# Warm-up matmuls: fifty of 256 columns for twenty-four of 512, in other banks and at one more place

## The chip, the cores and the metric

The kernel runs on one core of one Trainium2 chip. Its engines are TensorE (PE, with its weight loads listed as PEld), VectorE (DVE), ScalarE (ACT), GpSimd (POOL) and SyncE (SP), which here issues the DMAs. The metric is the device time of one execution in microseconds (us); lower is better.

## The reference

Two stages. First a gated linear attention over 768 steps for 4 batches of 8 heads with 48 channels: each head keeps a 48x48 state that is decayed by a sigmoid gate and takes in one outer product per step. Then a two-layer network on the 3072 tokens of 384 channels.

```python
def _attn_ref(q, k, v, f_logit):
    f = 1.0 / (1.0 + np.exp(-f_logit))
    state = np.zeros((B, H, D, D))
    for t in range(S):
        state = f[:, :, t, :, None] * state + np.einsum('bhd,bhe->bhde', k[:, :, t], v[:, :, t])
        y[:, :, t] = np.einsum('bhd,bhde->bhe', q[:, :, t], state)

def _moe_ref(x, w_in, w_out):
    h = x @ w_in                      # 3072 x 384 by 384 x 2048
    g = np.maximum(0.01 * h, h)
    return (g @ w_out)                # by 2048 x 384
```

## The kernel before, in words

The steps are cut into chunks of 128. There are twelve units of work: units 0 to 3 are the first two chunks of one batch each ("paired"), units 4 to 11 one later chunk of two batches. Each unit goes through the same steps:

- loads of f, k, q and v (`Lf`, `Lk`, `Lq`, `Lv`), all issued by SyncE in a fixed order;
- log gates on ScalarE (`ge` line 229, `gl` line 241);
- their prefix sums as matmuls with a triangular matrix (`cs`, lines 250 to 261), in paired units with a small addition on VectorE (`ca`, line 266);
- decay factors on ScalarE (`dec`, lines 274 to 280);
- k and q scaled by them (`k`, `q`, line 286) on VectorE or GpSimd, v cast on GpSimd (`v`, line 291);
- k and q turned, by transposes on TensorE (`tk`, `tq`, line 319) with copies on VectorE or ScalarE (`ck`, `cq`, lines 332 and 334), in later units by DMA (line 339);
- scores (`sc`, lines 355 and 362), masks on VectorE (`mk`, lines 372 and 376);
- the mix of scores and state (`mx`, `ms`, line 393) and the copy into xT (`xt`, lines 445 and 447);
- the state itself (`pt` line 458, `sf` lines 473 and 475, `sb` line 483);
- the network: up matmuls (`up` line 510 with 256 columns, `uw` line 521 with 512), the leaky ReLU on ScalarE (`pr`, `pw`, lines 516 and 525), down matmuls (`dn`, line 532), copies out and stores.

The two weight matrices are loaded in pieces (`We`, `WI`, `WO`) and cast to bf16 by three engines (`Ce`, `CI`, `CO`, lines 187 to 202).

Nothing schedules this at build time: one long list of words, `order`, is walked from left to right, and each word issues its step. So the list sets the order on every engine. A word such as `sc_1_0@6.7` says: the scores of unit 1, half 0, into PSUM banks 6 and 7. There are eight banks of 128 x 512 float32, given by hand. A step that writes a bank waits until the earlier contents have been read.

The word `F_7@1` means seven fills into bank 1. A fill (line 134) is a matmul of a constant tile with itself; nobody reads its result. Its bank counts like any other: the fill waits for the last reader of that bank.

Of the kernel before, what the change touches and what calls it, by code (L numbers as in the profile page):

```python
# [15 lines left out]
def kernel(  # L16
# [10 lines left out]
    nc = tc.nc  # L27
# [53 lines left out]
    banks = [psum.tile([128, 512], FP32, name=f"ps{i}", tag=f"ps{i}") for i in range(8)]  # L81
# [8 lines left out]
    filler = const.tile([128, 128], BF16, tag="filler")  # L90
# [40 lines left out]

    def fill(n, bank):
        for _ in range(n):
            nc.tensor.matmul(banks[bank].rearrange("t (a n) -> t a n", a=4), filler,  # L134
                             filler[:, None, :].to_broadcast([128, 4, 128]), start=True, stop=True)
# [349 lines left out]
    def wide(j):  # L485
        return j // 2 * 2 in WIDE
# [78 lines left out]
    def store(j, a):  # L565
# [46 lines left out]
    xt_5_1_1 mx_5_0@1 xt_5_0_1 dn_3_0_3 xt_4_0_0 uw_4_7@7 uw_4_9@4 pt_5_1@1 Lk_6_1 sf_4_1 ob_2_1_1 uw_4_4@2 pw_4_7
    Lf_8_0 Lk_6_0 uw_4_15@6 uw_4_0@7 pw_4_4 sf_4_0 uw_4_10@3 ob_3_1_0 uw_4_3@2 pw_4_9 pw_4_0 q_6_2_1 pw_4_10 ge_7_2
    uw_4_8@4 pt_5_0@7 sf_5_0 uw_4_12@5 uw_4_11@3 pw_4_3 uw_4_1@2 uw_4_2@7 pw_4_15 sb_4_1 gl_7_2 pw_4_8 pw_4_11 xq_6
    Lv_6_1 Lq_7_1 cs_7_1@6 cs_7_0@4 pw_4_1 pw_4_2 dec_7_1 uw_4_6@3 sb_5_0 sb_4_0 Lk_7_0 uw_4_13@2 sf_5_1 Lf_8_1
    Lq_7_0 dec_7_0 pw_4_6 st_1_0 k_6_2_0 pw_4_13 dn_4_1_0@1 uw_4_5@7 xk_6 q_7_2_0 pw_4_5 st_2_1 k_7_2_1 xk_7 Lv_6_0
# [64 lines left out]
```

## Time and profile before

| what | us |
|---|---|
| median of three runs | 179.84 |
| the three runs | 179.12, 179.84, 180.2 |
| the profiled execution, whole | 178.5 |
| its span, first to last instruction | 176.7 |
| TensorE busy in the span | 168.0 |
| ScalarE busy | 107.5 |
| VectorE busy | 79.1 |
| GpSimd busy | 72.7 |
| the 24 fills, busy | 9.2 |

The span is what the profile's rows are measured in; the whole execution is 1.8 us longer. An instruction is named by engine, line, operation and "out<-in" with tile names. PSUM banks all read `ps` there. Overlapping matmuls are pipelined, so a matmul's own duration is longer than the distance to the next one's start; costs of matmuls in a row are best read from the chain of waits, where each piece is only the time that it adds.

### The profile page before, as it was taken

How to read it: one execution, taken by the hardware profiler on the slowest of the kernel's cores; microseconds unless marked ns; L12 is line 12 of the kernel's file. 1: busy time of each engine (PE TensorE's matmuls, PEld its weight loads, DVE VectorE, ACT ScalarE, POOL GpSimd, SP SyncE). 2: the span in 40 equal slices, each digit the busy share in tenths (PEclk: the TensorE clock that was granted, in tenths of full speed). 3: DMA queues.
4: the chain of work that ended last, by engine and by line, in shares of the span. 5: the costliest groups of instructions: out<-in, count | busy, mean ns of one | idle time of the engine just before them, and what ended most of it. 6: DMA issues, size and time to landing. Idle time of an engine off the chain costs nothing.

```text
span 176.7 us, 5136 instructions
## 1 busy us (share of the span) xinstructions
PE 168.0 (95%) x2096; PEld 105.6 (60%) x2096; DVE 79.1 (45%) x166; ACT 107.5 (61%) x234; POOL 72.7 (41%) x151
## 2 busy tenths in 40 slices
PE   7698889999999999999999998999999999999993
PEld 2475668787566786754556744455754555644662
DVE  5259957802217333835128844506735355300030
ACT  4886964999155599269960687641799610378401
POOL 4687585532551745208525344802206980000000
PEclk9999999999999999999999999999999999999999
DMA  5999999499999499979999889999999990103004
GB/s 148 317 323 342 355 312 353 125 326 209 312 206 210 91 194 177 215 188 200 211 229 233 192 188 216 227 134 212 264 206 225 156 250 0 48 0 137 0 22 156
DMA packets 110407, 34.93 MB, mean 198 GB/s; under 512 B 102832, under 2 KB 109616, under 8 KB 110384
## 3 DMA queue, kind: packets, MB, share of 16 engines
q1 hardware_dynamic: 110384, 34.61, 84.1%
q8 instruction: 16, 0.26, 0.6%
q14 instruction: 7, 0.06, 0.1%
HBM read 25.17 MB, written 4.72 MB: 169 GB/s over the span
## 4 chain that ended last, share of the span: by engine, by line
PE 90%; DVE 3%; ACT 2%; DMA 2%; issue 1%; SPq 0%; DVEq 0%
PE ps L532 35%; PE ps L521 22%; PE ps L510 11%; PE ps L393 6%; PE ps L134 3%; PE ps L362 3%; DMA raw_fk<-in_f_logit_dram 2%; PE ps L319 2%; PE ps L548 2%; PE ps L258 1%; DVE wm L372 1%; PE ps L463 1%; PE ps L355 1%; PE ps L458 1%; PE ps L250 1%
## 5 line engine op out<-in xcount | busy, mean ns | idle before, releaser
L532 PE MATMUL ps<-w_out,gT 128*128 128x384 bf16 x368 | 66.1, 326 | 0.9 <-DVE sf L475 0.9
L532 PEld LDWEIGHTS <-gT 128*128 128x128 bf16 x368 | 34.4, 98 | 24.3 <-issue 1.2
L521 PE MATMUL ps<-xT,w_in 128*128 128x512 bf16 x192 | 45.2, 379 | 0.0
L525 ACT ACTIVATE gT<-ps 128x512 bf16<-128x512 f32 x64 | 34.5, 623 | 10.1 <-PE ps L521 9.6
L521 PEld LDWEIGHTS <-w_in 128*128 128x128 bf16 x192 | 18.1, 98 | 18.9
L376 DVE TENSOR_TENSOR wm<-ps,ut 128x512 bf16<-128x512 f32 x32 | 19.9, 684 | 17.0 <-PE ps L362 12.2
L286 POOL TENSOR_TENSOR qh<-raw_qv,at 128x768 bf16<-128x768 f32 (+1 forms) x10 | 14.0, 1404 | 24.3 <-ACT gT L525 9.4
L510 PE MATMUL ps<-xT,w_in 128*128 128x256 bf16 x192 | 22.9, 273 | 0.4 <-ACT xT L445 0.2
L516 ACT ACTIVATE gT<-ps 128x512 bf16<-128x512 f32 x32 | 17.9, 616 | 6.2 <-PE ps L510 6.2
L291 POOL CAST vb<-raw_qv 128x384 bf16<-128x384 f32 (+1 forms) x16 | 11.6, 723 | 23.6 <-DMA raw_qv<-in_v_dram 23.4
L510 PEld LDWEIGHTS <-w_in 128*128 128x128 bf16 x192 | 18.4, 98 | 3.6 <-DVE w_in L189 0.5
L483 POOL CAST sb<-sf 64x192 bf16<-64x192 f32 x40 | 14.9, 374 | 10.8 <-DVE sf L473 8.5
L445 ACT CAST xT<-ps 128x384 bf16<-128x384 f32 x15 | 7.8, 529 | 16.9 <-PE ps L393 13.5
L274 ACT ACTIVATE em<-ps 128x384 bf16<-128x384 f32 x24 | 12.2, 508 | 9.0 <-DVE wm L376 5.5
L229 ACT ACTIVATE e<-raw_fk 128x384 f32<-128x384 f32 (+1 forms) x16 | 11.0, 685 | 8.1 <-DMA raw_fk<-in_f_logit_dram 8.0
L286 DVE TENSOR_TENSOR kh<-raw_fk,em 128x768 bf16<-128x768 f32 (+1 forms) x10 | 9.0, 901 | 14.6 <-ACT em L274 9.7
L475 DVE TENSOR_TENSOR sf<-sf,ps 64x192 f32<-64x192 f32 x32 | 11.2, 351 | 6.4 <-ACT at L275 2.8
L543 DVE COPY osb<-ps 128x384 f32<-128x384 f32 x13 | 7.1, 554 | 13.0 <-PE ps L532 9.0
L275 ACT ACTIVATE at<-ps 128x384 bf16<-128x384 f32 x24 | 12.3, 512 | 0.0
L480 POOL TENSOR_TENSOR sf<-sf,end 128x192 f32<-128x192 f32 x16 | 8.9, 556 | 5.9 <-DVE sf L475 5.6
L372 DVE TENSOR_TENSOR wm<-ps,pair_mask 128x512 bf16<-128x512 f32 x16 | 10.4, 685 | 1.8 <-ACT lf L241 0.9
L134 PE MATMUL ps<-filler 128*128 128x512 bf16 x24 | 9.2, 511 | 2.0 <-DVE filler L93 1.1
(90 smaller groups left out, 180.2 us busy)
## 6 DMA issues: line engine op xcount, KB each, us to landing
out_dram<-osb SPq DMA_DIRECT2D x23, 192.0 KB, 3.1
raw_fk<-in_f_logit_dram SPq DMA_DIRECT2D x18, 192.0 KB, 3.8
raw_qv<-in_v_dram SPq DMA_DIRECT2D x18, 192.0 KB, 3.6
raw_fk<-in_k_dram SPq DMA_DIRECT2D x18, 192.0 KB, 3.7
raw_qv<-in_q_dram SPq DMA_DIRECT2D x18, 192.0 KB, 3.8
raw_fk<-in_moe_w_out_dram SPq DMA_DIRECT2D x2, 768.0 KB, 7.2
raw_qv<-in_moe_w_out_dram SPq DMA_DIRECT2D x2, 768.0 KB, 5.0
raw_fk<-in_f_logit_dram SPq DMA_DIRECT2D x3, 384.0 KB, 4.7
```

Source lines behind the costliest of these rows:

```text
L134: nc.tensor.matmul(banks[bank].rearrange("t (a n) -> t a n", a=4), filler, filler[:, None, :].to_broadcast([128, 4, 128]), start=True, sto ...
L274: nc.scalar.activation(ems[j % 2][:, a], t[:, 0:H * D], AF.Exp, scale=1.0)
L275: nc.scalar.activation(ats[j % 2][:, a], t[:, 0:H * D], AF.Exp, scale=-1.0)
L286: eng.tensor_mul(heads(j, to[j % NR], a)[:, :, :, 0:D], raw_heads(j, x, a), decays(j, by, a))
L372: nc.vector.tensor_mul(w.rearrange("t (s p) n -> t s p n", s=2), src.rearrange("t (s p n) -> t s p n", s=2, p=2), pair_mask[:, :, None, :] ...
L376: nc.vector.tensor_mul(w, src.rearrange("t (p n) -> t p n", p=P2), ut[:, None, :].to_broadcast([128, P2, 128]))
L483: nc.gpsimd.tensor_copy(out=sb[rows, :, y * D:y * D + D], in_=sf[rows])
L510: nc.tensor.matmul(pm[:, i, :], w_in_of(ff, kk), xTs[j // 2 % 2][:, kk, j % 2].rearrange("t a s -> t (a s)"), start=(kk == 0), stop=(kk == ...
L516: nc.scalar.activation(dst, pm, AF.Prelu, alpha=0.01)
L521: nc.tensor.matmul(banks[bank], w_in_of(ff, kk), xTs[j // 2 % 2][:, kk].rearrange("t u a s -> t (u a s)"), start=(kk == 0), stop=(kk == NK ...
L525: nc.scalar.activation(g_blocks(j)[ff], banks[st[j].pop(("pm", ff))], AF.Prelu, alpha=0.01)
L532: nc.tensor.matmul(po, g_of(j, ff, a), w_out_b[quarter][:, ff % 4, :], start=(ff == 0), stop=(ff == NF - 1))
```

## The change

A fill has 256 columns instead of 512. There are 50 fills instead of 24:

| place in the list, ahead of | before | after |
|---|---|---|
| first prefix sum of unit 0, `cs_0_1` | 7 in bank 1 | 21 in bank 1 |
| its second, `cs_0_0` | 3 in bank 2 | 3 in bank 2 |
| first of unit 1, `cs_1_0` | 3 in bank 3 | 5 in bank 3 |
| transposes `tk_1_1` | 4 in bank 5 | 7 in bank 4 |
| prefix sum `cs_2_1` | 2 in bank 1 | 3 in bank 3 |
| transposes `tq_1_0` | 1 in bank 4 | 2 in bank 4 |
| scores `sc_1_0` | 2 in bank 5 | 2 in bank 6 |
| mix `mx_1_2` | 2 in bank 2 | 3 in bank 5 |
| up matmuls `up_0_5` | none | 4 in bank 3 |

All other words stand in the same order. From `up_3_3` on, five of the eight banks are exchanged for each other (0 to 3, 1 to 2, 2 to 0, 3 to 5, 5 to 1), the same way to the end of the list; ahead of it only the fills' banks differ.

```diff
     def fill(n, bank):
         for _ in range(n):
-            nc.tensor.matmul(banks[bank].rearrange("t (a n) -> t a n", a=4), filler,
-                             filler[:, None, :].to_broadcast([128, 4, 128]), start=True, stop=True)
+            nc.tensor.matmul(banks[bank][:, 0:256].rearrange("t (a n) -> t a n", a=2), filler,
+                             filler[:, None, :].to_broadcast([128, 2, 128]), start=True, stop=True)
...
-    c0 Lf_0_1 ge_0_1 Lf_1_2 ge_1_1 gl_0_1 ge_1_0 zk_0 zv_0_0 zs_0_0 Lv_0_1 Lf_0_0 F_7@1 cs_0_1@0 ge_0_0 gl_0_0 Lk_0_1
+    c0 Lf_0_1 ge_0_1 Lf_1_2 ge_1_1 gl_0_1 ge_1_0 zk_0 zv_0_0 zs_0_0 Lv_0_1 Lf_0_0 F_21@1 cs_0_1@0 ge_0_0 gl_0_0
...
-    up_1_1@4 mk_2_0_1 sf_2_0 up_1_0@1 mk_2_1_1 Ce_1_0_1_1 pr_1_1 pr_1_0 mk_2_0_0 up_0_5@3 up_1_5@0 We_1_1 Lf_3_2
+    up_1_1@4 mk_2_0_1 sf_2_0 up_1_0@1 mk_2_1_1 Ce_1_0_1_1 pr_1_1 pr_1_0 mk_2_0_0 F_4@3 up_0_5@3 up_1_5@0 We_1_1
...
```

Three places as they stand in the program. In the rows `ps1_156` is bank 1 with a running number, `lf` the log gates, `bu` and `bs` the triangular matrices, `wm` the masked scores, `vb` the cast v, `kh` the scaled k, `w_in` the weights; `128x512` is the size of what is written.

TensorE, the last of the fills ahead of the first prefix sum and the first of those behind it, before:

```order
L134 LDWEIGHTS filler_170
L134 MATMUL ps1_156<-filler_170 128x512
L250 LDWEIGHTS bu_163
L250 MATMUL ps0_155<-lf0_78,bu_163 128x192
...
L255 MATMUL ps0_155<-half_ones_169,lf0_78 128x2
L134 LDWEIGHTS filler_170
L134 MATMUL ps2_157<-filler_170 128x512
```

The same place after the change:

```order
L134 LDWEIGHTS filler_170
L134 MATMUL ps1_156<-filler_170 128x256
L250 LDWEIGHTS bu_163
L250 MATMUL ps0_155<-lf0_78,bu_163 128x192
...
L255 MATMUL ps0_155<-half_ones_169,lf0_78 128x2
L134 LDWEIGHTS filler_170
L134 MATMUL ps2_157<-filler_170 128x256
```

The order is the same; the fills are half as wide, and the pair of weight load and fill is there 21 times instead of 7 ahead of `bu`.

TensorE, the fills between the state matmuls of unit 1 (L458) and its mix (L393), before:

```order
L458 MATMUL ps6_161<-vb1_96,kh1_82 128x96
L134 LDWEIGHTS filler_170
L134 MATMUL ps2_157<-filler_170 128x512
...
L393 LDWEIGHTS vb1_96
L393 MATMUL ps5_160<-wm4_109,vb1_96 32x128
```

After:

```order
L458 MATMUL ps6_161<-vb1_96,kh1_82 128x96
L134 LDWEIGHTS filler_170
L134 MATMUL ps5_160<-filler_170 128x256
...
L393 LDWEIGHTS vb1_96
L393 MATMUL ps5_160<-wm4_109,vb1_96 32x128
```

The fills went from bank 2, which held scores that a mask on VectorE reads, to bank 5, which held an earlier mix that ScalarE copied into xT and which the next mix writes.

TensorE, the up matmuls of unit 0 that read the third block of w_in, before:

```order
L510 LDWEIGHTS w_in0_171
L510 MATMUL ps1_156<-xT0_125,w_in0_171 128x256
L510 LDWEIGHTS w_in2_173
L510 MATMUL ps3_158<-xT0_125,w_in2_173 128x256
```

After:

```order
L510 LDWEIGHTS w_in0_171
L510 MATMUL ps1_156<-xT0_125,w_in0_171 128x256
L134 LDWEIGHTS filler_170
L134 MATMUL ps3_158<-filler_170 128x256
...
L510 LDWEIGHTS w_in2_173
L510 MATMUL ps3_158<-xT0_125,w_in2_173 128x256
```

Four fills now stand between the up matmuls on the first weight block and those on the third, in the bank that the latter write next.

More of the change, by code (lines that the diff above doesn't have):

```diff
@@ L612 @@
[L612 to L616, printed above, removed]
@@ new lines @@
+    pr_3_4 st_0_1 Lq_6_1 dn_2_1_3 v_4_2 ob_2_0_1 dn_3_1_1 cs_6_0@0 pr_3_7 v_5_2 dec_6_0 Lf_7_1 sc_5_0@2.5 sc_5_1@7.4
+    dn_3_1_2 mk_5_0_1 cs_6_1@5 mk_5_0_0 dn_3_0_0@3 dn_3_0_1 st_1_1 mk_5_1_0 sc_4_1@2.0 mk_5_1_1 sc_4_0@7.4 dec_6_1
+    mk_4_1_1 dn_3_0_2 pt_4_0@5 mk_4_1_0 mk_4_0_0 pt_4_1@0 dn_3_1_3 mk_4_0_1 mx_4_1@2 mx_4_0@7 mx_5_1@4 xt_4_1_1
+    xt_5_1_1 mx_5_0@2 xt_5_0_1 dn_3_0_3 xt_4_0_0 uw_4_7@7 uw_4_9@4 pt_5_1@2 Lk_6_1 sf_4_1 ob_2_1_1 uw_4_4@0 pw_4_7
+    Lf_8_0 Lk_6_0 uw_4_15@6 uw_4_0@7 pw_4_4 sf_4_0 uw_4_10@5 ob_3_1_0 uw_4_3@0 pw_4_9 pw_4_0 q_6_2_1 pw_4_10 ge_7_2
@@ new lines @@
+    dn_4_0_1 dn_4_1_1 dn_5_1_1 dn_4_0_2 sc_6_1@7.3 sc_6_0@1.0 Lf_11_1 dn_4_1_2 Lk_9_0 dn_4_1_3 mk_6_1_0 mk_6_1_1
+    mk_6_0_1 dn_5_0_1 dn_4_0_3 mk_6_0_0 ob_4_1_0 sc_7_1@7.3 sc_7_0@0.1 cs_8_0@2 dn_5_1_2 dn_5_0_2 Lv_8_1 mk_7_0_1
+    mk_7_0_0 mk_7_1_0 mk_7_1_1 cs_8_1@1 mx_6_1@0 dec_8_1 mx_6_0@7 mx_7_1@3 xt_6_0_0 mx_7_0@1 xt_7_1_0 pt_6_1@7
+    xt_6_1_1 xt_7_0_1 sf_6_1 dec_8_0 ge_9_2 sb_6_1 dn_5_0_3 pt_7_0@0 uw_6_14@3 uw_6_0@1 pw_6_0 pw_6_14 gl_9_2
+    uw_6_4@7 dn_5_1_3 uw_6_1@2 ob_5_1_0 pw_6_1 uw_6_8@1 cs_9_0@3 uw_6_3@5 pt_6_0@2 pw_6_4 sf_7_0 uw_6_2@0 ob_4_0_0
@@ new lines @@
+    pw_8_7 pw_8_0 pw_8_12 Lq_10_0 q_10_2_1 sb_9_0 v_10_2 pw_8_9 uw_8_10@3 Lv_11_1 Lq_11_0 Lk_11_1 st_7_0 uw_8_6@7
+    Lk_11_0 uw_8_11@1 uw_8_8@2 sf_9_1 k_10_2_0 uw_8_13@4 pw_8_8 pw_8_11 pw_8_10 pw_8_13 dn_8_0_0@6 xq_10 xk_10 sf_8_1
+    k_11_2_0 dn_9_1_0@5 dn_8_1_0@0 uw_8_15@2 q_11_2_1 pw_8_6 dn_9_1_1 dn_8_0_1 sc_10_0@1.3 sc_10_1@4.7 pw_8_15
+    dn_8_1_1 dn_8_0_2 xq_11 st_6_1 xk_11 dn_9_1_2 dn_9_0_0@2 dn_9_0_1 v_11_2 sb_8_0 sb_8_1 sb_9_1 st_7_1 mk_10_0_0
+    mk_10_1_0 mk_10_1_1 mk_10_0_1 sc_11_0@1.4 sc_11_1@7.3 dn_8_1_2 dn_8_0_3 dn_9_1_3 dn_9_0_2 mk_11_1_0 mk_11_0_1
@@ new lines @@
+    mk_11_0_0 mk_11_1_1 mx_11_1@7 mx_10_0@4 mx_10_1@1 mx_11_0@3 xt_11_1_1 dn_9_0_3 xt_10_1_0 xt_10_0_1 xt_11_0_1
+    ob_9_1_0 uw_10_8@7 uw_10_0@4 uw_10_2@1 dn_8_1_3 uw_10_5@3 pw_10_5 pw_10_0 ob_9_0_0 uw_10_6@5 pw_10_6 uw_10_4@2
+    uw_10_12@3 pw_10_4 uw_10_9@4 uw_10_1@5 st_6_0 uw_10_7@2 st_9_0 ob_8_0_1 uw_10_3@6 ob_8_1_1 pw_10_2 pw_10_8
+    pw_10_1 pw_10_7 uw_10_13@0 uw_10_10@1 pw_10_3 uw_10_11@7 uw_10_14@5 dn_11_0_0@2 st_8_1 st_8_0 pw_10_10 pw_10_11
+    pw_10_14 pw_10_13 pw_10_9 dn_10_0_0@6 uw_10_15@1 pw_10_12 dn_11_0_1 dn_10_1_0@7 dn_10_1_1 st_9_1 dn_10_0_1
```

67 lines of the change are left out of this document (26 added, 41 removed).

## The prediction

> **What bounds the kernel now.** I read the page first, then TensorE's timeline of the first 50 us, then the chain of waits up to 45 us, and last the timelines of ScalarE, VectorE and the DMA issues in the stretch where that chain leaves TensorE. From the page:
>
> ```profile
> span 176.7 us, 5136 instructions
> PEclk9999999999999999999999999999999999999999
> PE 90%; DVE 3%; ACT 2%; DMA 2%; issue 1%; SPq 0%; DVEq 0%
> L532 PE MATMUL ps<-w_out,gT 128*128 128x384 bf16 x368 | 66.1, 326 | 0.9 <-DVE sf L475 0.9
> L521 PE MATMUL ps<-xT,w_in 128*128 128x512 bf16 x192 | 45.2, 379 | 0.0
> L134 PE MATMUL ps<-filler 128*128 128x512 bf16 x24 | 9.2, 511 | 2.0 <-DVE filler L93 1.1
> ```
>
> TensorE carries 90% of the chain that ended last. The two big groups of real work, L532 and L521, lose 0.9 us in all to waits; so what moves the start of that work moves the end. The 24 fills (L134) compute nothing that is used. All the waits that matter are early:
>
> ```profile
> 1.05 3.17 PE L134 MATMUL ps<-filler 128*128 128x512 bf16 x7 [1.05 <-DVE filler L93]
> 5.80 0.32 PE L250 MATMUL ps<-lf,bu 128*128 128x192 bf16 x1 [1.57 <-ACT lf L241]
> ...
> 20.67 0.59 PE L134 MATMUL ps<-filler 128*128 128x512 bf16 x2 [0.50 <-DVE wm L372]
> ```
>
> Seven fills keep TensorE busy from 1.05 to 4.22; then it idles 1.57 us until the first log gates are there. The chain of waits (start, length, what) shows what follows:
>
> ```profile
> 5.33 0.42 ACT lf L241
> ...
> 6.68 1.30 PE ps L134 x3
> 7.98 0.16 PE ps L250
> 8.14 0.16 PE ps L251
> ...
> 8.71 1.29 PE ps L134 x3
> 10.00 0.08 PE ps L250
> 10.08 0.08 PE ps L251
> ...
> 20.67 0.59 PE ps L134 x2
> ...
> 22.03 0.60 ACT xT L445
> ...
> 23.43 0.45 issue
> ...
> 26.39 4.04 PE ps L510 x36
> ...
> 32.09 0.91 DVE w_in L189 x2
> 33.00 0.05 issue
> 33.05 6.07 PE ps L510 x54
> ```
>
> Two things are to be seen. First, the same 192-column matmul takes 0.16 us at 8.14 and 0.08 at 10.00: TensorE runs at half speed until about 9.9, although the page's clock row reads 9 throughout. It had then been busy without a gap since 5.80, 4.1 us; the 3.17 us of fills before the 1.57 us gap had not sufficed. Second, two fill groups of 1.3 us stand on the chain while half speed lasts, and one of 0.59 at 20.67, started when a mask had been read.
>
> **The change, part by part.**
>
> *The start, 21 fills of 256 columns for 7 of 512.* At half speed a fill takes 0.16 x 256/192 = 0.213 us, so 21 take 4.48 us: 1.05 to 5.53. The gap before 5.80 shrinks from 1.57 to 0.27 and the real work isn't delayed. When full speed then comes isn't shown. Bounds from the rows: at 1.05 + 4.1 = 5.1, if the small gap doesn't matter; at 9.9 as before, if any gap starts the count again. I take the early side, near 6.5 at the latest, since the gap left is a sixth of the old one.
>
> *Three and five small fills for 3 and 3 large ones.* At full speed they take 3 x 0.107 = 0.32 and 5 x 0.107 = 0.54 instead of 1.30 and 1.29. Then what is late next is ScalarE and VectorE:
>
> ```profile
> 6.81 0.52 ACT L241 ACTIVATE lf<-e 128x384 bf16<-128x384 f32 x1
> ...
> 8.04 0.94 ACT L241 ACTIVATE lf<-e 128x384 bf16<-128x384 f32 x2
> ...
> 10.45 0.49 ACT L274 ACTIVATE em<-ps 128x384 bf16<-128x384 f32 x1 [0.64 <-PE ps L255]
> ...
> 20.23 1.74 ACT L187 CAST w_in<-raw_fk 128x384 bf16<-128x384 f32 x4
> ```
>
> ```profile
> 9.39 0.59 DVE L286 TENSOR_TENSOR kh<-raw_fk,em 128x384 bf16<-128x384 f32 x1 [0.55 <-ACT em L274]
> 10.69 0.42 DVE L334 COPY kT<-ps 128x512 bf16<-128x512 bf16 x1 [0.71 <-PE ps L319]
> ...
> 12.08 0.74 DVE L473 TENSOR_TENSOR sf<-ps,end 64x192 f32<-64x192 f32 x2 [0.49 <-PE ps L458]
> ...
> 18.13 2.48 DVE L372 TENSOR_TENSOR wm<-ps,pair_mask 128x512 bf16<-128x512 f32 x4
> ```
>
> The second prefix sum waits for its log gates until 6.81 + 0.52 = 7.33 and the third until about 8.5 (half of the pair from 8.04); both are then done by 9, before VectorE ends the scaling of k at 9.98. ScalarE's 0.64 and VectorE's 0.71 and 0.49 of idle time, all waits for TensorE, go: VectorE gains up to 1.2 us by 12.08. From there it has hardly a gap:
>
> ```profile
> 10.00:12.00 2.00, 2.00 (x52) 1.82 (x53) 0.90 (x3) 1.55 (x5) 1.74 (x3) 1.00 1.16 323
> 12.00:14.00 2.00, 2.00 (x36) 1.44 (x36) 1.82 (x5) 1.83 (x6) 1.86 (x4) 1.00 1.17 325
> ...
> 16.00:18.00 2.00, 1.57 (x35) 0.91 (x41) 2.00 (x5) 1.26 (x5) 1.52 (x6) 1.00 1.09 365
> ...
> 20.00:22.00 2.00, 1.50 (x75) 0.92 (x70) 1.94 (x6) 1.97 (x5) 1.11 (x3) 1.00 1.07 353
> 22.00:24.00 2.00, 1.32 (x15) 0.96 (x15) 1.32 (x4) 0.59 (x1) 1.94 (x8) 1.00 0.97 288
> ```
>
> (The columns are the stretch, its length, then busy time of TensorE, its weight loads, VectorE, ScalarE, GpSimd, clock, DMA share, GB/s.) So from 12 to 22 VectorE sets the pace, and the fills there (7, 3, 2, 2, 3 small for 4, 2, 1, 2, 2 large, about a fifth fewer columns) lie beside it. The group at 20.67 no longer stands between the masks and the mix; that 0.59 is part of the same 1.2 and isn't added.
>
> *What caps this gain.* The last two of ScalarE's four weight casts from 20.23 read the load issued second, at 14.06:
>
> ```profile
> 14.06 0.49 SPq L180 DMA_DIRECT2D raw_fk<-in_moe_w_in_dram  x1
> raw_fk<-in_moe_w_in_dram SPq DMA_DIRECT2D x1, 384.0 KB, 6.2
> ```
>
> It lands at 14.06 + 6.2 = 20.3. The loads are issued in a fixed order with the DMA share above 1, and nothing in the change brings them earlier. The third cast started at 20.23 + 0.87 = 21.1, so it can move 0.75 us at most, and the copy of xT at 22.03, behind it on ScalarE, with it. Term: -0.75, between -0.8 and, if full speed stays at 9.9, -0.5: the fills are then 0.64 and 1.07 long, the third prefix sum ends at 9.9 instead of 10.4, and VectorE gains 0.5.
>
> *Four new fills before the up matmuls that read the third weight block.* They stand inside the 36 matmuls from 26.39, which run without a wait, 4.04/36 = 0.112 each. Four more of the same width cost 4 x 0.112 = +0.45 (0 if the casts for that block were late; they shift with everything else, so I take all of it). That delays the mix, the copy of xT and the casts at 32.09 on which 33.05 waits.
>
> *New banks from the last ups of the third unit on.* The rest of the order is the old one with banks renamed; only at the seam do waits differ. There the second prefix sum of a later unit now needs the bank that the first mask reads:
>
> ```profile
> 69.05 2.48 DVE L376 TENSOR_TENSOR wm<-ps,ut 128x512 bf16<-128x512 f32 x4 [3.50 <-PE ps L362]
> ```
>
> ```profile
> 69.76 0.33 PE L258 MATMUL ps<-lf,ut 128*128 128x384 bf16 x1
> ```
>
> That mask, one of four of 0.62 to 0.7 us, ends at about 69.74; the prefix sum came at 69.76. Term: +0.05 (0 to 0.1).
>
> **The sum.** -0.75 + 0.45 + 0.05 = -0.25 us on the profiled execution's 178.5: 178.25. The median of the runs is 179.84, 1.34 above the profiled execution, and even the fastest run, 179.12, is 0.62 above. I keep those 0.62 and let the other 0.72, which differ from run to run, go: 178.25 + 0.62 = 178.9. The reason is that TensorE is busy 2.00 of 2.00 us from 10 to 14, so each us by which full speed comes later costs half a us, and the change takes this stretch off the chain. Keeping none or all of the 1.34 gives 178.25 and 179.6.
>
> [...]
>
> **Rivals.**
>
> 1. *All of the runs' excess is a late full clock.* A clock that is 2.7 us later costs 2.7/2 = 1.34 in the busy stretch from 9.9. Once the fills cover the start, none of it is left: 178.25, say 178.3. For it: the spread of 1.08 us between three runs of one program. Against: even the fastest run is 0.62 off. Chance 0.15.
>
> 2. *No earlier clock.* The 0.27 us gap counts like the old one. Then -0.5 + 0.45 + 0.05 = 0, and the runs keep their excess: 179.8. For it: 3.17 us of fills were no help before. Chance 0.26.
>
> 3. *The stall at 23.43 goes.* Nothing that the profile shows ended these 0.45 us, between transposes of one group; with 22 more fills ahead it may fall elsewhere, into idle time: 178.9 - 0.45 = 178.4. Chance 0.06.
>
> 4. *The clock falls back (slower).* Fewer fill columns and earlier fills leave TensorE more idle from 12 to 24 us. If half speed returns about 24 and lasts 4 us as at the start, the dense work from 24 on takes 4/2 = 2.0 us longer: 180.9. It decides where TensorE's busy share falls below what was enough before; the lowest such stretch, 22 to 24, has 1.32/2.00 = 66%, and full speed held (0.112 for 256 columns at 26.39). Against it: that stretch itself has no fills to lose. Chance 0.08.
>
> My forecast has the remaining 0.45, with a range of its own from 178.5 to 179.3.
>
> **How the numbers follow.** About 0.5% (0.9 us) is what this measurement can tell, so faster means below 178.94. Of the forecast's 0.45 some 0.27 lies below it; rivals 1 and 3 add 0.15 and 0.06: 0.48. The same: 0.18 of the forecast and rival 2, 0.44. Slower: rival 4, 0.08. The range from 178.0 to 180.0 takes in rivals 1, 2 and 3 with their bounds and leaves out rival 4 and the tails.
>
> **What would show it.** In the changed kernel's timeline: the first prefix sum still at about 5.8, after a gap of 0.3; its 192-column matmuls or the next group's at 0.08 spacing; no VectorE idle of 0.7 before the kT copy; the xT copy near 21.3 instead of 22.03; four fills of 0.45 in a row near 27; the 54 ups starting about 0.3 earlier than 33.05. I am wrong if the spacing stays 0.16 up to 9.9, if 33.05 doesn't move, or if a gap opens between 33 and 110 us.

## The result: 1.25% slower, and where the profile after puts the time

In alternating runs on one chip, 15 of each kernel, the median went from 178.87 us (176.85 to 181.3) to 181.2 us (178.95 to 182.96): a ratio of 1.0125, 95% interval 1.0079 to 1.017. (Ratios here and below leave out runs that are more than 1.5% above the fastest of their kernel, so they can differ a little from the quotient of the medians.) The profiled execution of the changed kernel took 182.12 us, its span 180.3, 3.6 more than the 176.7 before; the medians lie 2.3 apart, so this execution shows the loss somewhat too large.

From the page of the changed kernel (the clock row is in tenths of full speed, 40 slices of 4.5 us; the third line is the share of each engine in the chain that ended last; the fourth gives packets, MB and share of a DMA queue):

```profile
span 180.3 us, 5190 instructions
PEclk9999969999999999999999999999999999999999
PE 79%; DMA 7%; SPq 4%; issue 3%; ACT 3%; DVE 1%; DVEq 0%; ACTq 0%
q8 instruction: 16, 0.26, 0.6%
```

TensorE's share of the chain fell from 90% to 79%, "issue" rose from 1% to 3%, and one slice near 25 us has a lowered clock. TensorE's timeline of the same kernel (start, length, what, idle before and its releaser):

```profile
1.05 4.66 PE L134 MATMUL ps<-filler 128*128 128x256 bf16 x21 [1.05 <-DVE filler L93]
5.71 0.32 PE L250 MATMUL ps<-lf,bu 128*128 128x192 bf16 x1
...
20.08 0.28 PE L393 MATMUL ps<-wm,v 64*32 64x128 bf16 x5
23.62 0.31 PE L393 MATMUL ps<-wm,v 64*32 64x128 bf16 x11 [3.26 <-issue]
23.86 0.43 PE L319 MATMUL ps<-ident,kh 128*128 128x128 bf16 x4
```

The start went as intended: the 21 fills reach without a gap to the first prefix sum. Then TensorE stands still for 3.26 us in the middle of a mix, five matmuls done and eleven to go, all reading and writing the same tiles. The profile names no engine and no data that it waits for. The chain of waits (start, length, what) shows the same, and how far the rest has moved:

```profile
20.36 3.26 issue
23.62 0.34 PE ps L393 x10
...
30.52 0.44 PE ps L134 x4
...
36.03 6.07 PE ps L510 x54
...
70.69 4.98 DMA qT<-qh
75.81 0.62 PE ps L362 x16
```

The 54 up matmuls that started at 33.05 start at 36.03. Busy time by stretch (stretch, length, then busy us of TensorE, its weight loads, VectorE, ScalarE, GpSimd, then clock, DMA share, GB/s) shows the second loss:

```profile
20.70:24.10 3.40, 0.48 (x16) 0.38 (x16) 1.25 (x4) 1.13 (x4) 2.35 (x8) 1.00 1.03 361
24.10:27.50 3.40, 3.29 (x22) 2.42 (x20) 1.87 (x5) 1.55 (x3) 2.01 (x6) 0.50 1.11 363
```

After a stretch in which TensorE was busy 0.48 of 3.40 us, the clock is granted at 0.50 for the next 3.4 us. In 13 of the 15 runs of this kernel the mean granted clock was 0.991 or lower; one stretch of 3.4 us at half speed gives 1 - 1.7/180.3 = 0.991. Of 29 runs of the kernel before, beside the first experiments, 6 were as low.

The same matmul, fills aside, can be found in both traces. How much later it starts in the changed kernel:

| time in before | what | lag, us |
|---|---|---|
| 5.80 | first prefix sum | -0.09 |
| 9.80 | third | -1.19 |
| 19.66 | state matmuls of unit 1 | -0.93 |
| 21.19 | mix of unit 1, `mx_1_2` | -1.59 |
| 21.93 | next transposes, behind the stall | +1.92 |
| 26.39 | the 36 ups, in the half-speed stretch | +2.72 |
| behind the four new fills | ups of units 0 and 1 | +3.15 |
| 33.05 | the 54 ups | +2.98 |
| 71.4 | scores of unit 4 | +4.39 |
| 110.87 | down matmuls | +3.22 |
| 176.7 | end | +3.6 |

So 1.59 us were gained; the stall and what directly follows it took 3.51, half speed 0.80, the four fills 0.43, and 0.17 came back. The last rows are later waits that exchange places: at 75.81 TensorE waits 1.29 us for a transposing DMA that it did not wait for before, and the wait of 0.9 for VectorE (L475) behind 110 us is gone.

**The stall is an old one.** The before kernel's chain has "issue" at 23.43 for 0.45 us, likewise between matmuls of one step; its timeline there:

```profile
23.22 0.22 PE L319 MATMUL ps<-ident,qh 128*128 128x128 bf16 x1
23.88 0.33 PE L319 MATMUL ps<-ident,qh 128*128 128x128 bf16 x3 [0.45 <-issue]
```

Counting weight loads and matmuls in TensorE's order, both stalls come ahead of the same number, row 704. A fill is two rows. The before kernel has 24 fills ahead of that point, the changed one 46: 22 x 2 = 44 rows more, so row 704 falls 44 rows earlier in the real work, out of the transposes of unit 2 into the mix of unit 1. The page has a queue that may carry instructions: q8, which it calls "instruction", moves 16 packets and 0.26 MB, 16 KB each. TensorE has 4244 weight loads and matmuls in the trace; if the packets carry them that is about 62 bytes each, an estimate from these two figures. The second of these packets, in stretches of 0.1 us around its start (packets, MB, its time as a share of 16 engines over the stretch), before:

```profile
q8 instruction: 1, 0.02, 59.9%
```

and in the changed kernel, from 21.3 to 21.4:

```profile
q8 instruction: 1, 0.02, 60.0%
```

0.60 x 16 engines x 0.1 us is 0.96 us for the one packet. By the trace's records it goes from 21.63 to 22.59 before and from 21.35 to 22.31 after. TensorE resumes at 23.88 and at 23.62: 1.29 and 1.31 us behind its end.

### The profile page after: what moved, and what is told of

It is laid out like the page before. It is cut to its first block, busy times and chain, and to the rows that moved or that the text cites. A ratio compares the mean times of both kernels' runs of the same rounds, so it can differ in the third digit from the quotient of the medians.

```text
span 180.3 us, 5190 instructions
## 1 busy us (share of the span) xinstructions
PE 169.9 (94%) x2122; PEld 109.1 (60%) x2122; DVE 79.2 (44%) x166; ACT 107.4 (60%) x234; POOL 71.6 (40%) x151
## 4 chain that ended last, share of the span: by engine, by line
PE 79%; DMA 7%; SPq 4%; issue 3%; ACT 3%; DVE 1%; DVEq 0%; ACTq 0%
PE ps L532 29%; PE ps L521 23%; PE ps L510 10%; PE ps L393 6%; SPq L164 3%; DMA raw_fk<-in_f_logit_dram 3%; DMA qT<-qh 3%; PE ps L362 2%; DMA kT<-kh 2%; PE ps L548 1%; PE ps L463 1%; PE ps L258 1%; SPq L339 1%; PE ps L355 1%; PE ps L319 1%
## 5 line engine op out<-in xcount | busy, mean ns | idle before, releaser
L521 PEld LDWEIGHTS <-w_in 128*128 128x128 bf16 x192 | 18.2, 98 | 18.9
L510 PE MATMUL ps<-xT,w_in 128*128 128x256 bf16 x192 | 24.3, 280 | 0.1
L286 POOL TENSOR_TENSOR qh<-raw_qv,at 128x768 bf16<-128x768 f32 (+1 forms) x10 | 14.6, 1458 | 21.9 <-ACT gT L525 10.8
L510 PEld LDWEIGHTS <-w_in 128*128 128x128 bf16 x192 | 18.9, 100 | 3.8 <-issue 0.4
L475 DVE TENSOR_TENSOR sf<-sf,ps 64x192 f32<-64x192 f32 x32 | 11.2, 351 | 7.7 <-PE ps L463 4.1
L393 PE MATMUL ps<-wm,v 64*32 64x128 bf16 (+1 forms) x256 | 8.5, 218 | 3.3 <-issue 3.3
L480 POOL TENSOR_TENSOR sf<-sf,end 128x192 f32<-128x192 f32 x16 | 8.1, 505 | 7.8 <-DVE sf L475 7.5
```

Of the source, the lines that this page charges most:

```text
L286: eng.tensor_mul(heads(j, to[j % NR], a)[:, :, :, 0:D], raw_heads(j, x, a), decays(j, by, a))
L393: nc.tensor.matmul(banks[st[j]["py", i]][32 * r:32 * r + 32, 128 * kk:128 * kk + 128], lhsT, rhs, start=(i, r) not in begun, stop=i in las ...
L510: nc.tensor.matmul(pm[:, i, :], w_in_of(ff, kk), xTs[j // 2 % 2][:, kk, j % 2].rearrange("t a s -> t (a s)"), start=(kk == 0), stop=(kk == ...
L521: nc.tensor.matmul(banks[bank], w_in_of(ff, kk), xTs[j // 2 % 2][:, kk].rearrange("t u a s -> t (u a s)"), start=(kk == 0), stop=(kk == NK ...
```

## The experiments

*Theory 1*, a guess of the author from the count of rows and from q8: ahead of row 704 TensorE has run out of instructions. The next ones come as a packet through the DMA engines that are full of loads (DMA share 1.03 from 20.70 to 24.10). So the number of fills ahead, two instructions each, sets where TensorE stalls and for how long; half speed follows from the stall. Form 1a: the packet is late because it shares the DMA engines with the loads. Form 1b: it comes when it comes, whatever the loads do. *Rivals:* the new places and banks make the wait; or fewer fill columns leave TensorE too idle and the clock falls of itself.

The fills of the kernels, as count of words `F` by place (columns per fill in the head):

| ahead of | before, 512 | after, 256 | twice, 256 | wide, 512 | few, 512 | start11, 512 | lean, 512 | balanced, 512 |
|---|---|---|---|---|---|---|---|---|
| `cs_0_1` | 7 | 21 | 14 | 11 | 11 | 11 | 11 | 11 |
| `cs_0_0` | 3 | 3 | 6 | 2 | 0 | 3 | 0 | 1 |
| `cs_1_0` | 3 | 5 | 6 | 3 | 0 | 3 | 0 | 2 |
| `tk_1_1` | 4 | 7 | 8 | 4 | 0 | 4 | 4 | 4 |
| `cs_2_1` | 2 | 3 | 4 | 2 | 0 | 2 | 2 | 2 |
| `tq_1_0` | 1 | 2 | 2 | 1 | 0 | 1 | 1 | 1 |
| `sc_1_0` | 2 | 2 | 4 | 1 | 0 | 2 | 1 | 1 |
| `mx_1_2` | 2 | 3 | 4 | 2 | 0 | 2 | 0 | 2 |
| ahead of row 704 | 24 | 46 | 48 | 26 | 11 | 28 | 19 | 24 |
| `up_0_5` | 0 | 4 | 0 | 2 | 0 | 0 | 0 | 0 |
| places and banks of | before | after | before | after | before | before | after | after |

And what was measured, with the stall at row 704 and the second packet of q8 by each trace:

| kernel | stall, us | packet 2 | half speed after it | 54 ups start | ratio of runs (95%) |
|---|---|---|---|---|---|
| before | 23.43 to 23.88 | 21.63 to 22.59 | none | 33.05 | 1 |
| after | 20.36 to 23.62 | 21.35 to 22.31 | 24.09 to 27.50 | 36.03 | 1.0125 (1.0079 to 1.017) |
| twice | 22.11 to 24.94 | 22.50 to 23.47 | 23.99 to 30.81 | 37.97 | 1.0201 (1.0113 to 1.0288) |
| wide | 22.06 to 22.30 | 20.00 to 20.95 | none | 32.17 | 0.9967 (0.9923 to 1.0011) |
| few | none | 20.99 to 21.87 | 16.38 to 19.79 (ahead of it) | 31.88 | 1.0009 (0.9972 to 1.0047) |
| start11 | 22.56 to 24.12 | 21.74 to 22.67 | 24.92 to 28.34 | 35.28 | 0.9959 (0.9914 to 1.0004) |
| lean | 22.74 to 23.66 | 21.29 to 22.25 | 23.38 to 30.20 | 35.64 | 1.001 (0.9967 to 1.0054) |
| balanced | 22.89 to 23.35 | 21.02 to 21.99 | none | 32.59 | 0.9919 (0.9876 to 0.9961) |

**Twice: the before kernel with each fill split in two.** Places, banks and columns as before, 48 instructions more ahead of the point.

```diff
-            nc.tensor.matmul(banks[bank].rearrange("t (a n) -> t a n", a=4), filler,
-                             filler[:, None, :].to_broadcast([128, 4, 128]), start=True, stop=True)
+            nc.tensor.matmul(banks[bank][:, 0:256].rearrange("t (a n) -> t a n", a=2), filler,
+                             filler[:, None, :].to_broadcast([128, 2, 128]), start=True, stop=True)
...
-    Ce_0_1_1_1 F_2@2 mx_1_2@5.4 k_2_0_0 tk_2_0@1 sf_1_0 cq_2_0_0 Ce_0_0_0_1 Ce_0_0_1_1 xt_1_0_1 up_0_1@2 k_2_1_1
+    Ce_0_1_1_1 F_4@2 mx_1_2@5.4 k_2_0_0 tk_2_0@1 sf_1_0 cq_2_0_0 Ce_0_0_0_1 Ce_0_0_1_1 xt_1_0_1 up_0_1@2 k_2_1_1
...
```

> Each fill of the kernel before is split into two of 256 columns in the same bank at the same place: the same columns and waits, 24 more pairs of weight load and matmul, all ahead of TensorE's row 704 (the instruction at which it stood still for 0.45 us before and for 3.26 us after the change). Theory 1 (TensorE runs out of instructions at that row, which arrive at a time of their own): the stall is at row 704 again, that is 48 rows earlier in the work, inside the mix of unit 1, and 1.5 to 3.5 us long; the 54 up matmuls start 1 to 3 us later than 33.05; time 0.6 to 1.8% above the kernel before. Theory 2 (the clock falls back because fewer fill columns leave TensorE idle): no change, within 0.3%. Theory 3 (the four new fills and the new banks cost it): no change, within 0.3%.

Median 182.98 against 179.04. TensorE's timeline of this kernel:

```profile
21.83 0.27 PE L393 MATMUL ps<-wm,v 64*32 64x128 bf16 x3
24.94 0.43 PE L393 MATMUL ps<-wm,v 64*32 64x128 bf16 x13 [2.83 <-issue]
```

The same step is cut, now 3 to 13 instead of 5 to 11: two fills more ahead than in the changed kernel, four rows, two pairs of weight load and matmul earlier. The loss is larger than expected: half speed lasts 6.82 us and the 54 ups come 4.92 later, not 1 to 3. But neither a new place nor a new bank nor a missing column is needed for the loss; the number of instructions is enough.

**Wide: the changed kernel with 28 fills of 512 columns for its 50 of 256.** All its places and banks are kept.

```diff
-            nc.tensor.matmul(banks[bank][:, 0:256].rearrange("t (a n) -> t a n", a=2), filler,
-                             filler[:, None, :].to_broadcast([128, 2, 128]), start=True, stop=True)
+            nc.tensor.matmul(banks[bank].rearrange("t (a n) -> t a n", a=4), filler,
+                             filler[:, None, :].to_broadcast([128, 4, 128]), start=True, stop=True)
...
-    Ce_0_1_0_1 Ce_0_1_1_1 F_3@5 mx_1_2@5.4 k_2_0_0 tk_2_0@1 sf_1_0 cq_2_0_0 Ce_0_0_0_1 Ce_0_0_1_1 xt_1_0_1 up_0_1@2
+    Ce_0_1_0_1 Ce_0_1_1_1 F_2@5 mx_1_2@5.4 k_2_0_0 tk_2_0@1 sf_1_0 cq_2_0_0 Ce_0_0_0_1 Ce_0_0_1_1 xt_1_0_1 up_0_1@2
...
```

> The changed kernel with its places and banks, but 28 fills of 512 columns instead of 50 of 256 (11, 2, 3, 4, 2, 1, 1, 2, 2): about the same columns, 22 pairs of instructions fewer. Theory 1: row 704 is only four rows earlier in the work than before; full speed early as in the changed kernel; the stall at row 704 is 0.5 to 1.7 us and too short to bring half speed back; time within 0.4% of the kernel before, 1% below the changed one. Theory 2: half speed comes back as in the changed kernel, 0.8 to 1.5% slower than before. Theory 3: the four fills' columns and the banks are still there, 0.8 to 1.5% slower than before.

Median 178.77 against 179.04, the loss is gone. Its timeline, its chain and a stretch of its busy times:

```profile
20.53 0.40 PE L319 MATMUL ps<-ident,kh 128*128 128x128 bf16 x4 [0.44 <-DVE kh L286]
22.30 0.27 PE L510 MATMUL ps<-xT,w_in 128*128 128x256 bf16 x1 [0.24 <-issue]
```

```profile
32.17 6.07 PE ps L510 x54
```

```profile
20.00:23.40 3.40, 2.29 (x32) 1.75 (x24) 2.91 (x8) 1.98 (x5) 2.41 (x9) 1.00 1.03 342
```

TensorE stalls two fills' worth of rows ahead of the before kernel's place, for 0.24 us, less than the 0.5 to 1.7 expected; the stretch that held the long stall is 67% busy and the clock stays. The 54 ups come 0.88 earlier than before, so the start and the shorter groups bring more than the prediction's 0.3, once the instructions are not doubled.

**Few: eleven fills at the start and no others.** The before kernel with its other fill words taken out.

```diff
-    c0 Lf_0_1 ge_0_1 Lf_1_2 ge_1_1 gl_0_1 ge_1_0 zk_0 zv_0_0 zs_0_0 Lv_0_1 Lf_0_0 F_7@1 cs_0_1@0 ge_0_0 gl_0_0 Lk_0_1
+    c0 Lf_0_1 ge_0_1 Lf_1_2 ge_1_1 gl_0_1 ge_1_0 zk_0 zv_0_0 zs_0_0 Lv_0_1 Lf_0_0 F_11@1 cs_0_1@0 ge_0_0 gl_0_0 Lk_0_1
...
-    gl_2_0 sf_0_0 ck_0_0_0 F_4@5 tk_1_1@4 tk_1_0@5 cs_2_0@7 sb_0_0 ge_2_1 cq_0_0_0 mk_0_1_1 ck_1_1_1 mk_0_1_0 ca_2_0
+    gl_2_0 sf_0_0 ck_0_0_0 tk_1_1@4 tk_1_0@5 cs_2_0@7 sb_0_0 ge_2_1 cq_0_0_0 mk_0_1_1 ck_1_1_1 mk_0_1_0 ca_2_0
...
```

> The kernel before with 11 fills of 512 columns at the start and no other fills. Theory 1: row 704 is 26 rows later in the work than before; no stall there or one below 0.5 us; full speed from about 6 to 7 us; the 54 up matmuls start at 32.0 to 32.5 instead of 33.05; 0.3 to 0.6% faster than before. Theory 2: with no fills after the start TensorE is idle more than ever, half speed comes back between 12 and 24 us, 0.8 to 1.5% slower. Theory 3: nothing of the four fills and banks, so 0 to 0.4% faster.

Median 179.06 against 179.04, the same. There is no stall at row 704, which here lies 26 rows later in the work. Instead half speed returns earlier:

```profile
13.00:16.40 3.40, 1.89 (x53) 1.64 (x50) 3.40 (x9) 2.83 (x8) 1.28 (x4) 1.00 1.16 332
16.40:19.80 3.40, 3.40 (x124) 2.47 (x112) 3.00 (x6) 2.13 (x7) 3.40 (x8) 0.50 0.97 279
```

56% busy, no idle time over 0.63 us in it, and the next 3.4 us are at half speed. In ten of the twelve runs the mean clock was 0.99 or lower. Of the 29 runs of the kernel before, 6 were at 0.991 or lower. So in these runs the fills between the steps do hold the clock: this part of theory 2 came true, its 0.8 to 1.5% did not. The 54 ups still start 1.17 earlier than before. That lead is 0.77 at 96 us and 1.41 at 119 us, and by 151 us the kernel is 0.25 behind. A wait of 0.73 for a transposing DMA (kT, at 142.89) is a part of that; the rest was not taken apart. Here 1.17 us gained early were worth nothing at the end.

**Start11: the before kernel with 11 instead of 7 fills at the start.** Four fills more, eight rows.

```diff
-    c0 Lf_0_1 ge_0_1 Lf_1_2 ge_1_1 gl_0_1 ge_1_0 zk_0 zv_0_0 zs_0_0 Lv_0_1 Lf_0_0 F_7@1 cs_0_1@0 ge_0_0 gl_0_0 Lk_0_1
+    c0 Lf_0_1 ge_0_1 Lf_1_2 ge_1_1 gl_0_1 ge_1_0 zk_0 zv_0_0 zs_0_0 Lv_0_1 Lf_0_0 F_11@1 cs_0_1@0 ge_0_0 gl_0_0 Lk_0_1
...
```

> The kernel before with 11 instead of 7 fills of 512 columns at the start, nothing else. Theory 1: full speed comes early, TensorE is 0.5 to 1 us earlier at row 704 but the instructions aren't: a stall of 0.8 to 1.8 us; no half speed after it; time within 0.3% of the kernel before. Theories 2 and 3: the earlier start is kept in part, 0.2 to 0.5% faster.

Median 178.43 against 179.04, the interval just reaches 1; by time alone theories 2 and 3 (0.2 to 0.5% faster) fit as well as theory 1. What decides is the stall. The profiled execution, 180.6, is one of the longer ones: it has a stall of 1.57, then 3.4 us of half speed, which theory 1 had not expected; of the other eleven runs ten had a mean clock of 0.999 or more.

```profile
24.12 0.49 PE L510 MATMUL ps<-xT,w_in 128*128 128x256 bf16 x3 [1.57 <-issue]
```

Four more fills move the stall by eight rows, as they should. TensorE goes on 1.45 us behind the end of the packet, and the moment of the packet differs between executions: 21.35 and 21.67 in two of the changed kernel, with stalls of 3.26 and 3.67 us. That the half speed behind the stall differs with it is a guess.

**Without the later weight loads.** To see whether the packet waits for the loads, the changed kernel was run without the loads and casts of three of the four blocks of `w_in` and a constant in their place.

```diff
+        "F": fill, "mw": lambda i: nc.vector.memset(w_in_b[i], 0.01),
...
-    cq_1_0_1 mk_0_0_1 tq_1_1@4 We_0_0 q_2_0_0 cq_1_1_1 v_1_0 dec_2_1 Lv_2_2 WI_2 F_2@6 sc_1_0@6.7 mx_0_2@5.1
+    cq_1_0_1 mk_0_0_1 tq_1_1@4 We_0_0 q_2_0_0 cq_1_1_1 v_1_0 dec_2_1 Lv_2_2 F_2@6 sc_1_0@6.7 mx_0_2@5.1
...
```

> The changed kernel without the loads and casts of three quarters of the second-stage weights w_in (blocks 1 to 3 are set to a constant instead, so the up matmuls compute with wrong weights): the DMA queue has less outstanding between 16 and 24 us, TensorE's instructions are the same. Theory 1a (the instructions for row 704 come late because they are fetched by the same DMA engines behind the loads): the second instruction packet ends before 21.5 instead of 22.3, the stall at row 704 shrinks from 3.3 us to below 2, half speed does not come back. Theory 1b (the fetch has a time of its own, whatever the loads do): packet and stall as in the changed kernel, 2.8 to 3.5 us.

```profile
PE ps L393 <- issue: 2.7, 1, 2.7
```

(The waits of this kernel's TensorE: total, times, longest.) 2.7 us lies between the two forms, the packet (20.54 to 21.50) ends just where form 1a set its bound, and half speed came back (23.14 to 26.55), which form 1a excluded: inconclusive. The edit was too weak; from 20 to 21 us the DMA share was still 1.18. One run, 181.83.

**Lean: fills of 512 columns only where half speed was expected to threaten.** It was meant to be better than both kernels.

```diff
-    Ce_0_1_0_1 Ce_0_1_1_1 F_3@5 mx_1_2@5.4 k_2_0_0 tk_2_0@1 sf_1_0 cq_2_0_0 Ce_0_0_0_1 Ce_0_0_1_1 xt_1_0_1 up_0_1@2
+    Ce_0_1_0_1 Ce_0_1_1_1 mx_1_2@5.4 k_2_0_0 tk_2_0@1 sf_1_0 cq_2_0_0 Ce_0_0_0_1 Ce_0_0_1_1 xt_1_0_1 up_0_1@2
...
```

> The second experiment's kernel with 19 of its 28 fills of 512 columns: without those in front of the second and third prefix sums, the second mix and the third weight block. Row 704 is ten rows later in the work than before. Theory 1: no stall at row 704 above 0.3 us; full speed from 4.5 to 7.5 us on, kept through 24 us as the fills between 11 and 17 us are still there; the 54 up matmuls start at 31.7 to 32.2; 0.4 to 0.9% faster than the kernel before. Rival (the fills that are left out were what held the clock): half speed comes back between 16 and 24 us and the time is within 0.3% of the kernel before.

Ratio 1.001, medians 180.72 against 179.69: no gain. In nine of its twelve runs the mean clock was 0.991 or lower. Its timeline and two stretches:

```profile
22.47 0.27 PE L319 MATMUL ps<-ident,kh 128*128 128x128 bf16 x2
23.66 0.37 PE L319 MATMUL ps<-ident,kh 128*128 128x128 bf16 x2 [0.92 <-issue]
```

```profile
20.00:23.40 3.40, 1.63 (x24) 1.20 (x17) 2.58 (x7) 2.14 (x5) 2.44 (x9) 1.00 1.02 357
23.40:30.20 6.80, 6.54 (x82) 4.57 (x82) 4.00 (x10) 2.92 (x6) 2.92 (x8) 0.50 1.01 329
```

The stall sits where five fills fewer than before must put it, five matmuls with their weight loads later. But 48% busy did not hold the clock, and 6.8 us went by at half speed, as the rival about missing fill columns had it. The stall has a part in those 48%, for 0.66 of its 0.92 us lies in that stretch; the kernel with few fills, which has no stall, is the clean sign that missing fills alone can bring half speed back. A theory of instructions alone would go too far.

**The changed kernel again**, with no edit, beside the next one.

> The changed kernel once more, as a control of its one profile. Theory 1: the stall is at row 704 again, 2.5 to 3.5 us, and half speed follows it for 3.4 us or more. Rival (the stall was one execution's accident): no stall above 0.5 us.

```profile
PE ps L393 <- issue: 3.7, 1, 3.7
```

The stall is there again, at the same matmul (20.25 to 23.92, behind a packet from 21.67 to 22.63), and half speed follows from 23.65 to 27.06; one run, 184.9.

**A pause in the loads.** The changed kernel, with four loads held back behind a small copy on SyncE that waits for the last mask of unit 1. TensorE's instructions are the same ones; the file is five lines longer, so L398 is L393 here and L324 is L319.

```diff
+    def gate():
+        nc.sync.dma_start(out=gate_tile, in_=wms[6][:, 0, :])
...
-    sc_1_1@2.4 mk_1_0_1 mk_1_0_0 v_1_1 tq_2_0@7 q_2_1_1 mk_1_1_1 mk_1_1_0 xt_0_0_1 ms_0 pt_1_2@3.6 xt_0_1_1
+    sc_1_1@2.4 mk_1_0_1 mk_1_0_0 v_1_1 tq_2_0@7 q_2_1_1 mk_1_1_1 mk_1_1_0 bar We_0_1 We_0_0 Lv_2_2 WI_2 xt_0_0_1 ms_0 pt_1_2@3.6 xt_0_1_1
...
```

> The changed kernel with a pause in the loads: behind the last load of k for unit 2, SyncE first issues one small copy that waits for the last mask of unit 1 (about 19.6 us), and only then the first two loads of w_in, the last load of v and the next block of w_in (they come later in the list than before; the computation is the same). The DMA engines run empty from about 18 to 20 us; TensorE's instructions are those of the changed kernel. Theory 1a (the instructions are fetched late because the DMA engines are full of loads): the second instruction packet starts before 19 us instead of 21.4, and the stall at row 704 is below 0.8 us instead of 3.3; the casts and the xT copy behind the late loads come 2 to 4 us later instead. Theory 1b (the fetch takes its time whatever the loads do): packet at 21 to 21.7, stall 2.7 to 3.7 us.

The stall at row 704 is gone. First the busy times of the changed kernel (the last two columns are DMA share and GB/s), then of this one, then its q8 from 18.0 to 18.2 and its TensorE timeline:

```profile
17.00:18.00 1.00, 1.00 (x88) 0.87 (x80) 1.00 (x3) 1.00 (x5) 1.00 (x4) 1.00 0.96 290
18.00:19.00 1.00, 1.00 (x46) 0.70 (x36) 1.00 (x2) 0.70 (x2) 1.00 (x4) 1.00 0.93 309
```

```profile
17.00:18.00 1.00, 1.00 (x80) 0.80 (x79) 1.00 (x3) 1.00 (x5) 0.70 (x3) 1.00 0.14 37
18.00:19.00 1.00, 1.00 (x40) 0.77 (x32) 1.00 (x3) 0.70 (x2) 1.00 (x5) 1.00 0.08 19
```

```profile
q8 instruction: 1, 0.02, 36.3%
```

```profile
19.97 0.71 PE L398 MATMUL ps<-wm,v 64*32 64x128 bf16 x16
20.61 0.40 PE L324 MATMUL ps<-ident,kh 128*128 128x128 bf16 x4
```

With the DMA engines at 0.14 and 0.08 instead of 0.96 and 0.93, packet 2 starts at 18.00 instead of 21.35 and ends at 19.16, and the mix that was cut 5 to 11 runs through all 16. That is what form 1a expected: with the loads held back, the packet comes 3.35 us sooner and the stall of 3.26 us is gone. TensorE itself is no later or earlier up to there: its 527th row, at which the packet starts in the probe, comes at 18.00 there and at 18.11 in the changed kernel. One execution of the probe stands against two of the changed kernel. The kernel as a whole is slower (one run, 185.32), because what was held back is missed later: TensorE waits 5.00 us for a cast (`L515 <- ACT w_in L192`), 2 to 4 were expected, and half speed comes back behind that wait, from 24.06 to 30.89. It is a probe and no remedy.

The pages of the kernels before and after count 16 packets of q8 each. Even so, in each of the eleven traces at most one idle time of TensorE over 0.2 us ends in "issue", the one ahead of row 704. Nine traces stall there, for 0.24 to 3.67 us. The two others are the probe with the pause, where packet 2 is over at 19.16 and the cut mix starts at 19.97, and few fills, where it is over at 21.87 and TensorE, by count of rows, gets to row 704 at 23.76, 1.89 us later.

**Balanced: the changed kernel's places and banks, 512 columns, and as many fills as before.** 24 fills put row 704 where it was before; the fills taken out are the ones between the first prefix sums, and those from `tk_1_1` on stay, to hold the clock.

```diff
-    c0 Lf_0_1 ge_0_1 Lf_1_2 ge_1_1 gl_0_1 ge_1_0 zk_0 zv_0_0 zs_0_0 Lv_0_1 Lf_0_0 F_21@1 cs_0_1@0 ge_0_0 gl_0_0
-    Lk_0_1 Lv_0_0 zk_2 dec_0_1 v_0_1 Lq_0_1 Lk_0_0 Lq_0_0 zk_1 F_3@2 cs_0_0@1 zs_1_0 Lk_1_2 gl_1_0 gl_1_1 k_0_1_0
-    F_5@3 cs_1_0@2 Lf_2_2 dec_0_0 q_0_1_0 k_0_0_0 pm_1 tk_0_1@3 tq_0_1@4 cs_1_1@5 dec_1_0 v_0_0 tk_0_0@6 ck_0_1_0
+    c0 Lf_0_1 ge_0_1 Lf_1_2 ge_1_1 gl_0_1 ge_1_0 zk_0 zv_0_0 zs_0_0 Lv_0_1 Lf_0_0 F_11@1 cs_0_1@0 ge_0_0 gl_0_0
+    Lk_0_1 Lv_0_0 zk_2 dec_0_1 v_0_1 Lq_0_1 Lk_0_0 Lq_0_0 zk_1 F_1@2 cs_0_0@1 zs_1_0 Lk_1_2 gl_1_0 gl_1_1 k_0_1_0
+    F_2@3 cs_1_0@2 Lf_2_2 dec_0_0 q_0_1_0 k_0_0_0 pm_1 tk_0_1@3 tq_0_1@4 cs_1_1@5 dec_1_0 v_0_0 tk_0_0@6 ck_0_1_0
...
```

> The changed kernel's places and banks with 24 fills of 512 columns (11, 1, 2, 4, 2, 1, 1, 2, and none in front of the third weight block): as many instructions ahead of row 704 as in the kernel before. Theory 1: full speed early, stall at row 704 below 1 us, half speed does not come back in most executions; 0.3 to 0.7% faster than the kernel before. Rival (half speed returns as in the sixth experiment): within 0.3%.

Median 178.09 (176.48 to 180.57) against 179.42, ratio 0.9919 (0.9876 to 0.9961): faster than before, and the only kernel here whose interval lies below 1. Its timeline and two stretches:

```profile
22.67 0.22 PE L319 MATMUL ps<-ident,qh 128*128 128x128 bf16 x1
23.35 0.33 PE L319 MATMUL ps<-ident,qh 128*128 128x128 bf16 x3 [0.46 <-issue]
```

```profile
20.00:23.40 3.40, 1.80 (x59) 1.27 (x44) 2.95 (x7) 1.59 (x4) 2.47 (x8) 1.00 1.01 347
23.40:30.20 6.80, 6.80 (x157) 5.67 (x156) 4.66 (x10) 4.10 (x8) 3.23 (x10) 1.00 1.08 371
```

The stall cuts the very group that it cuts in the before kernel, one transpose done and three to go, for 0.46 us; the clock holds at 53% busy, and in eleven of its twelve runs the mean clock was 0.998 or more. In its profiled execution the 54 ups start 0.46 earlier and the span is 0.3 shorter; the medians differ by 1.3. Where the other 1.0 comes from is not shown by one trace.

## Why the prediction was wrong

It named 178.9 us, and a chance of 0.08 for slower. Step by step:

- *The start.* Right. The fills end at 5.71, the first prefix sum isn't delayed, and by the trace full speed comes at 7.02 instead of 9.86, half a us later than the "near 6.5 at the latest" of the text. No row of the traces gives that 6.5. In the second execution of the changed kernel full speed comes at 6.58, so the moment does move between runs.
- *Small fill groups and the engines behind them.* Right in sign, short in size: 1.59 us were gained by the mix of unit 1, where up to 1.2 was named, and 0.75 of it was to survive the landing of a weight load. The lead was 0.93 at the state matmuls of unit 1, and 0.66 came on top at the mix, whose fills no longer wait for a mask: the 0.59 that the text counted as part of the same 1.2. The load landed at 20.86 in the changed kernel (20.28 before), but TensorE already stood still, so the cap never decided.
- *Four new fills, +0.45.* 0.43 by lag, 0.44 in the chain.
- *New banks, +0.05.* 0.04: the lag grows from 3.00 to 3.04 at the prefix sum that the text names. (Three words at the seam are not renamed by the rule of the rest: `up_3_3` goes from bank 0 to 5, `cs_6_0` from 1 to 0, and the second bank of `sc_5_0` from 0 to 5.)
- **The step that failed** is the pricing of the fills by their columns alone, and with it rival 3. The fills from `tk_1_1` on were put "beside" VectorE's work at no cost, "about a fifth fewer columns"; the 22 instruction pairs more had no price. The stall at 23.43, "nothing that the profile shows ended", was taken as something that might vanish (chance 0.06). It was the one sign in the profile of before of what the change would run into: it is bound to the instruction's number (row 704 in all nine traces that stall), comes 44 rows earlier in the work, and grew: TensorE reached the number at 20.36 instead of 23.43, 3.07 us sooner, while the packet ended only 0.28 sooner. 0.45 + 3.07 - 0.28 = 3.24, and 3.26 were measured.
- *Rival 4, the clock falls back near 24.* It came, from 24.09 to 27.50, but behind the stall (TensorE was busy 0.48 of 3.40 us), and not through the missing columns as argued. It cost 0.80 where 2.0 was named; 3.4 us of dense work would have lost 1.7, but the kernel before keeps TensorE busy only 66% from 22 to 24 us. That its 180.9 lies near the measured 181.2 is chance: the larger part was the stall.
- *Rival 1, all of the runs' excess is a late full clock.* The balanced kernel has eleven wide fills at the start, and in its trace full clock comes early (the distance from fill to fill falls from 0.43 to 0.22 us at about 4.5), yet its runs still spread over 4.1 us, and over 2.5 without the two longest. That speaks against it; when full speed came in each of those runs was not recorded.
- *Rival 2, no earlier clock.* Refuted by 7.02 and 6.58.

What the forecast was right about is seen in the wide kernel, the same places and banks with about half the fills: the 54 ups 0.88 earlier, 175.8 us of span, and a ratio of 0.9967. Only, its interval reaches 1, so that gain is not settled.

## What to carry to other kernels

Here a filler cost instructions as well as columns. With the DMA share at 1.03 from 20.70 to 24.10, TensorE went on 1.31 us behind the end of the second packet of q8, which came only 0.28 us sooner than before, while 22 pairs of weight load and matmul more in front of row 704 and the quicker start brought TensorE there 3.07 us sooner. A short idle time in the middle of one step, which the profile ends with "issue", is worth a count of the engine's instructions up to it in two kernels; if the number is the same, try fewer and wider instructions ahead of it (here that took the stall from 3.26 to 0.24 us). Fills still had to be there to hold the clock: with 11 or 19 of them ahead of row 704 half speed came back for 3.41 and 6.82 us and nothing was gained (ratios 1.0009 and 1.001), and 24 wide ones, no more than before, were the fastest here (0.9919). Widen them rather than split them: the fills of the kernel before, split in two, gave 1.0201.

## What was not expected of the hardware

- The second 16 KB packet of instructions took 0.88 to 1.16 us, and TensorE went on 1.29 to 1.47 us after its end in every trace that stalled. It started at 20.00 to 22.50 in the ten traces without a pause in the loads (DMA share 1.03 in the changed kernel from 20.70 to 24.10), and at 18.00 in the pause, with shares of 0.14 and 0.08. What sets its place between 20.00 and 22.50 is not shown.
- Half speed returned after stretches of 3.4 us that were far from idle: 47% busy (start11, from 21.50), 48% (lean) and 56% (few); the stall lies in the first two. It lasted 3.41 us (after, few) or 6.82 (twice, lean). 53% in the balanced kernel kept full speed, so a busy share over stretches placed as here does not give the bound; it stays open.
- Which instructions a packet carries no row shows. That q8 serves TensorE is inferred from its size and from the stalls, which end 1.29 to 1.47 us behind its second packet.
